# Linear attention with a gated feed-forward on one core: F by the casting queue, first scores ahead of the turns of F, last unit normalised by VectorE

## The chip, the cores and the metric

The kernel runs on one core of one Trainium2 chip. The time is the device time of an execution in microseconds (us); a profile's span is about 1.8 us shorter than the time of the same execution.

## The reference

```python
k_proj = np.einsum('ks,bhsd->bhkd', E, k)            # E, F: [64, 1024], b = h = 8, s = 1024, d = 64
v_proj = np.einsum('ks,bhsd->bhkd', F, v)
scores = scale * np.matmul(q, k_proj.transpose(0, 1, 3, 2))
attn = softmax(scores)                               # over 64 columns
x = np.matmul(attn, v_proj)                          # -> [8192, 512]
g = x @ w_gate; val = x @ w_val                      # 512 -> 1536
out = (g * sigmoid(g) * val) @ w_out                 # 1536 -> 512, float32
```

## The kernel before

The work of one chunk of 512 tokens follows on that of the last; TensorE does attention for a later chunk between feed-forward matmuls. All of that is the same in both kernels. The change touches the prologue, in which nothing is loaded yet. Its parts (cuts marked with `...`):

```python
# loads. nc.sync / nc.scalar: hardware queues. nc.gpsimd: the queue that casts fp32 to bf16
nc.scalar.dma_start(out=kraw[i][:], in_=k[0, 2*i : 2*i+2]...)      # i = 0, 1: heads 0-3, fp32
nc.sync.dma_start(out=Eraw, in_=E); nc.scalar.dma_start(out=Fraw, in_=F)    # fp32 (condensed)
load_q(0, 0, (0, 2)); load_k(0, 4, 8)                              # casting queue
...
load_q(0, 0, (2, 4)); load_v(0, (0, 4, 6, 8)); load_w_gv(0, 1); load_w_gv(1, 2, (0,))
warm(11); turn(0, "v"); warm(4)      # fillers; E turned by TensorE
...
u_KV(0, "k", (0, 4), at="y")         # project k of heads 0-3
u_T(0, 0, "a", act)                  # turn q of unit 0
u_KT0((0, 2), "vg", ...)             # block-diagonal k
turn(1, "a", (0,))                   # F, half 0
u_T(0, 2, "a", act)
u_S(0, 0, "g"); u_R(0, 0); u_N(0, 0) # scores+exp (ACT), row sums (VectorE), normalise (GpSimd)
load_w_gv(1, 2, (1,)); load_w_gv(2, 4, (0,))       # GpSimd issues these behind u_N(0, 0)
...
u_S(0, 2, "g"); u_A(0, 0, dve)       # turn the attention tile of unit 0, copied by VectorE
u_R(0, 2); u_N(0, 2)
u_S(0, 1, "g"); ...; u_N(0, 1); u_S(0, 3, "v"); ...; u_N(0, 3)
u_V0(0, 2, "y"); u_PV2(0, 0, 0, 0, act); ...       # project v, then attention times v
load_w_gv(2, 4, (1,))                # GpSimd: behind u_N(0, 3)
f_mm(0, 0, 0, 0); ...                # first feed-forward matmuls
load_w_gv(4, 6); load_q(0, 1, hs=(0, 4)); load_w_gv(6, 8); ...
```

`load_w_gv(c0, c1)` loads the columns of w_gate and w_val of the feed-forward tiles c0 to c1-1. A chunk uses tile f's w_gate, then w_val, and goes on to f + 1. GpSimd takes its work in order, so a casting DMA waits for the normalisation ahead of it (in the profile before, GpSimd normalises until 20.05 us and its next DMA issue starts at 20.00). A unit is one quarter of the first chunk's attention: four heads, half of the chunk's tokens. A "turn" is a transpose on TensorE, and a piece is the columns that one weight DMA brings.

The softmax here doesn't subtract the row's maximum and nothing guards it: scores larger than these inputs give would overflow.

## Time and profile before

| | before |
|---|---|
| median of the first 3 runs | 569.97 us (569.49 to 570.03) |
| profiled execution | 569.27 us, span 567.5 us |
| TensorE busy | 561.1 us (99%) |
| TensorE 46 to 560 us | 100% |
| granted clock | 0.999 |

The profile's page starts with the busy time per engine. A time line gives one row per group of like instructions: start, duration, engine, source line, operation, output <- input, and in brackets the idle time before it with what ended it. The lists of waits give who waited for whom, total us, times, longest. In these lines PE is TensorE, PEld its weight loads, DVE VectorE, ACT ScalarE, POOL GpSimd, and SPq the queue of SyncE.

### The profile page before, as it was taken

The numbers are of one execution on the slowest core, as the hardware profiler recorded it, in microseconds if no ns is written. First come the engines' busy times: TensorE is split into PE (matmuls) and PEld (weight loads), VectorE is DVE, ScalarE is ACT, GpSimd is POOL, SyncE is SP. The second block draws the span as 40 slices with busy tenths as digits, with TensorE's granted clock in tenths as the row PEclk, the third lists the DMA queues.
The fourth block names the chain that finished last, engine by engine and source line by source line (L and its number), as shares of the span: only waits on it lengthen the run. The fifth ranks groups of instructions, "written<-read, shape, count | busy, mean of one in ns | idle before, by whom it ended". The sixth has DMA issues, their size and how long they took to land.

```text
span 567.5 us, 7942 instructions
## 1 busy us (share of the span) xinstructions
PE 561.1 (99%) x2970; PEld 266.5 (47%) x2970; DVE 338.9 (60%) x576; ACT 235.7 (42%) x416; POOL 111.0 (20%) x124
## 2 busy tenths in 40 slices
PE   8999999999999999999999999999999999999997
PEld 4654444444444444444444444444444444444444
DVE  3786664766476645766466655666547665545550
ACT  3564452444435443443434434354343543443322
POOL 6951250124012400123002230023100220000000
PEclk9999999999999999999999999999999999999999
DMA  9999999729913795029940499106990213101012
GB/s 207 184 199 190 168 146 199 138 57 185 194 49 74 116 198 114 38 57 166 182 80 37 76 185 203 38 19 112 192 180 19 61 39 69 38 37 38 19 38 93
DMA packets 111159, 62.91 MB, mean 111 GB/s; under 512 B 64272, under 2 KB 102416, under 8 KB 111120
## 3 DMA queue, kind: packets, MB, share of 16 engines
q0 software_dynamic: 42816, 29.36, 36.1%
q1 hardware_dynamic: 67392, 31.46, 26.6%
q10 hardware_dynamic: 912, 1.57, 1.0%
q8 instruction: 23, 0.38, 0.3%
q14 instruction: 16, 0.13, 0.1%
HBM read 60.29 MB, written 16.78 MB: 136 GB/s over the span
## 4 chain that ended last, share of the span: by engine, by line
PE 95%; DMA 2%; POOL 1%; DVE 1%; ACT 0%; issue 0%; POOLq 0%
PE yps L415 29%; PE vps L377 28%; PE gps L377 28%; PE kvp L150 3%; PE sc L271 2%; PE pv L328 2%; DMA wv<-in_moe_w_val_dram 2%; PE warm L517 1%; PE efp L505 0%; POOL AA L301 0%; POOL wv L118 0%; POOL wg L118 0%; DVE BD L138 0%; PE kTp L194 0%; PE qTp L237 0%
## 5 line engine op out<-in xcount | busy, mean ns | idle before, releaser
L396 DVE SCALAR_TENSOR_TENSOR s<-th,gps 128x512 f32<-128x512 f32 x192 | 130.4, 679 | 134.6 <-ACT th L389 134.1
L377 PE MATMUL vps<-xT,wv 128*128 128x512 bf16 (+1 forms) x776 | 197.5, 377 | 0.4 <-DMA wv<-in_moe_w_val_dram 0.3
L377 PE MATMUL gps<-xT,wg 128*128 128x512 bf16 (+1 forms) x776 | 197.7, 377 | 0.1
L415 PE MATMUL yps<-wo,hT 128*128 128x512 bf16 (+1 forms) x780 | 194.5, 376 | 0.0
L389 ACT ACTIVATE th<-gps 128x512 f32<-128x512 f32 x192 | 114.6, 597 | 159.0 <-PE gps L377 153.9
L401 DVE TENSOR_TENSOR hT<-s,vps 128x512 bf16<-128x512 f32 x192 | 132.0, 687 | 20.4 <-DVE s L396 0.5
L301 POOL TENSOR_TENSOR AAd<-ee,rr 128x512 bf16<-128x512 f32 x56 | 58.3, 1043 | 342.3 <-issue 184.8
L415 PEld LDWEIGHTS <-hT 128*128 128x128 bf16 x780 | 76.2, 98 | 89.9
L377 PEld LDWEIGHTS <-wv 128*128 128x128 bf16 x776 | 73.8, 98 | 84.2 <-issue 2.9
L377 PEld LDWEIGHTS <-wg 128*128 128x128 bf16 x776 | 74.0, 98 | 81.3 <-issue 1.2
L425 ACT ACTIVATE ysb<-yps 128x512 f32<-128x512 f32 (+1 forms) x65 | 38.4, 591 | 77.7 <-PE yps L415 77.7
L138 ACT CAST xT<-pv 128x512 bf16<-128x512 f32 (+1 forms) x62 | 35.9, 582 | 52.3 <-PE pv L328 50.3
L286 DVE TENSOR_REDUCE zz<-ee 128x8 f32<-128x512 f32 x64 | 43.5, 679 | 22.4 <-ACT ee L275 22.4
L275 ACT ACTIVATE ee<-sc 128x512 f32<-128x512 f32 x64 | 37.9, 595 | 19.7 <-PE sc L271 18.5
L271 PEld LDWEIGHTS <-qTd 128*128 128x128 bf16 x224 | 17.2, 98 | 13.2 <-DMA qTd<-qb 0.2
L328 PE MATMUL pv<-AT,BDV 128*128 128x512 bf16 x60 | 22.4, 379 | 0.1
L271 PE MATMUL sc<-BD,qTd 128*128 128x128 bf16 x224 | 21.6, 219 | 0.0
L288 DVE RECIPROCAL rr<-zz 128x8 f32<-128x8 f32 x64 | 13.0, 203 | 6.7 <-DVE zz L286 0.5
L108 POOL DMA_DIRECT2D qb<-in_q_dram x18 | 16.3, 908 | 1.4 <-POOLq L655 0.8
L150 PE MATMUL kvp<-kb,ET 128*64 128x512 bf16 (+1 forms) x72 | 15.5, 358 | 0.0
L162 DVE CAST BDV<-kvp 64x256 bf16<-64x256 f32 x7 | 3.0, 426 | 20.0 <-ACT ks L158 17.8
L150 PE MATMUL kvp<-vb,FT 128*64 128x512 bf16 x56 | 13.4, 382 | 0.0
(64 smaller groups left out, 137.7 us busy)
## 6 DMA issues: line engine op xcount, KB each, us to landing
out_dram<-ysb SPq DMA_DIRECT2D x63, 256.0 KB, 2.3
qb<-in_q_dram POOLq DMA_DIRECT2D x14, 512.0 KB, 18.0
kb<-in_k_dram POOLq DMA_DIRECT2D x7, 1024.0 KB, 11.0
vb<-in_v_dram POOLq DMA_DIRECT2D x7, 1024.0 KB, 14.4
wo<-in_moe_w_out_dram POOLq DMA_DIRECT2D x2, 768.0 KB, 21.8
wg<-in_moe_w_gate_dram POOLq DMA_DIRECT2D x5, 256.0 KB, 8.0
wv<-in_moe_w_val_dram POOLq DMA_DIRECT2D x5, 256.0 KB, 9.6
kraw<-in_k_dram ACTq DMA_DIRECT2D x2, 512.0 KB, 4.9
```

What stands on the lines that cost most here:

```text
L138: (nc.scalar.copy if eng is nc.scalar else eng.tensor_copy)(out=out, in_=in_)
L150: nc.tensor.matmul(out=t[lo : lo + 64, h0:h1].rearrange("p h d -> p (h d)"), lhsT=w[:, j, :], rhs=src[b][:, h0:h1, j, :], start=(j == 0), ...
L271: nc.tensor.matmul(out=ps[:, n, :], lhsT=t[:, n, :], rhs=BD[b % 2][:, 4 * g + n, :], start=True, stop=True)
L275: nc.scalar.activation(out=e[:].rearrange("p h j k -> p (h j k)"), in_=ps[:].rearrange("p a k -> p (a k)"), func=AF.Exp, scale=scale,)
L286: nc.vector.reduce_sum(out=z[:], in_=e[:], axis=AX.X)
L301: eng.tensor_tensor(out=a.rearrange("p j h k -> p h j k"), in0=ee.pop((b, u))[:], in1=rr.pop((b, u))[:].unsqueeze(3).to_broadcast([P, 4, 2 ...
L377: nc.tensor.matmul(out=ps[:, ts], lhsT=(wg, wv)[w][:, kt, f * P : (f + 1) * P], rhs=x[:, kt, ts], start=(kt == 0), stop=(kt == NKT - 1),)
L389: nc.scalar.activation(out=th[:], in_=ps[:], func=AF.Tanh, scale=0.5)
L396: nc.vector.scalar_tensor_tensor(out=s1[:], in0=th[:], scalar=1.0, in1=g[:], op0=ALU.add, op1=ALU.mult)
L401: nc.vector.tensor_tensor(out=hT[c][:, f, :], in0=s1[:], in1=ps[:], op=ALU.mult)
L415: nc.tensor.matmul(out=yy[c][:, cs], lhsT=hT[c][:, f, i * P : (i + 1) * P], rhs=wo[:, f, cs], start=(f == 0), stop=(f == NFT - 1),)
L425: nc.scalar.activation(out=ysb[:, cs], in_=yy[c][:, cs], func=AF.Copy, scale=0.5)
```

## The change

Four intents: the fp32 load of F leaves ACT's hardware queue and comes as bf16 by the casting queue, between q and v, so that k, E and q land sooner; F's turns move behind the second scores, where they no longer hold up the first exp; the last of the four normalisations goes to VectorE, so that GpSimd is through earlier; and the copy of the first attention tile moves from VectorE to ACT.

```diff
-        ef = []
-        for which, src in (("E", E), ("F", F)):
-            raw = const.tile([KP, S], FP32, name=f"{which}raw")
-            (nc.sync if which == "E" else nc.scalar).dma_start(out=raw[:], in_=src)
-            ef.append(raw)
+        ef = [const.tile([KP, S], dt, name=f"{n}raw") for n, dt in (("E", FP32), ("F", BF16))]
+        nc.sync.dma_start(out=ef[0][:], in_=E)
...            # turn(): PSUM tile and identity in bf16 for F
         load_q(0, 0, (2, 4))
+        nc.gpsimd.dma_start(out=ef[1][:], in_=F)
         load_v(0, (0, 4, 6, 8))
...
         u_KV(0, "k", (0, 4), at="y")
-        warm(1)
         u_T(0, 0, "a", act)
         u_KT0((0, 2), "vg", (dve, dve, dve, act))
-        turn(1, "a", (0,))
-        u_T(0, 2, "a", act)
+        warm(1)
         u_S(0, 0, "g")
...
-        turn(1, "a", (1,))
-        warm(1)
+        u_T(0, 2, "a", act)
+        warm(2)
         u_KV(0, "k", (4, 8), at="y")
...
         u_S(0, 2, "g")
-        u_A(0, 0, dve)
         u_R(0, 2)
         u_N(0, 2)
+        turn(1, "a", (0,))
         u_S(0, 1, "g")
         u_R(0, 1)
         u_N(0, 1)
+        turn(1, "a", (1,))
         u_S(0, 3, "v")
         u_R(0, 3)
-        u_N(0, 3)
+        u_A(0, 0, act)
+        u_N(0, 3, dve)
...            # one warm(1) less; u_A(0, 1, dve) and u_A(0, 3, act) a few places earlier
```

More of the change, by code (lines that the diff above doesn't have):

```diff
@@ L501, in turn @@
             for half in halves:
-                ps = bank(at, [P, 4, KP], FP32, "efp")
+                ps = bank(at, [P, 4, KP], (FP32, BF16)[which], "efp")
                 for i in range(4):
-                    j = 4 * half + i
                     nc.tensor.transpose(
                         out=ps[:, i, :],
-                        in_=ef[which][:, bass.ds(j, P, step=NJ)],
-                        identity=ident_fp[:KP, :KP],
+                        in_=ef[which][:, bass.ds(4 * half + i, P, step=NJ)],
+                        identity=(ident_fp, ident_bf)[which][:KP, :KP],
                     )
@@ L562 @@
         u_N(0, 1)
+        turn(1, "a", (1,))
         u_S(0, 3, "v")
         u_R(0, 3)
-        u_N(0, 3)
+        u_A(0, 0, act)
+        u_N(0, 3, dve)
         u_V0(0, 2, "y")
         u_PV2(0, 0, 0, 0, act)
-        warm(1)
         u_V0(2, 3, "y")
@@ L572 @@
         u_PV1(0, 0, 2, 0, dve)
+        u_A(0, 1, dve)
         u_PV1(0, 0, 3, 0, act)
-        u_A(0, 1, dve)
+        u_A(0, 3, act)
         load_w_gv(2, 4, (1,))
         f_mm(0, 0, 0, 0)
-        u_A(0, 3, act)
         u_PV2(0, 0, 0, 1, dve)
```

## The prediction

> **What bounds the kernel now.** I read the page's list of busy times first, then the busy tenths, then TensorE's waits, then the time line of the start. The page of the kernel before:
>
> ```profile
> span 567.5 us, 7942 instructions
> ...
> PE 561.1 (99%) x2970; PEld 266.5 (47%) x2970; DVE 338.9 (60%) x576; ACT 235.7 (42%) x416; POOL 111.0 (20%) x124
> ```
>
> TensorE is busy for 99% of the span, so 567.5 - 561.1 = 6.4 us are left, and some of those 561 us are fillers ("warm" matmuls that keep the clock up). Where TensorE waits for a named thing (waits of TensorE, whole span; us in total, times, longest):
>
> ```profile
> PE warm L517 <- DVE zeros L495: 1.2, 1, 1.2
> PE pv L343 <- ACT BDV L185: 0.5, 1, 0.5
> PE vps L377 <- DMA wv<-in_moe_w_val_dram: 0.3, 1, 0.3
> PE pv L355 <- ACT AT L138: 0.2, 1, 0.2
> ```
>
> All lie before 22 us. The busy table by stages gives TensorE 100% of every stretch from 46 us to 560 us. That part is a fixed amount of work: what the change can gain, it gains before some 35 us, and the rest moves as a block. So the question is what sets the pace there. The time line of TensorE has these starts (start us, us, then the group; the last bracket is idle time and what ended it):
>
> ```profile
> 12.47 1.06 PE L150 MATMUL kvp<-kb,ET 128*64 128x256 bf16 x8
> ...
> 21.21 0.61 PE L377 MATMUL vps<-xT,wv 128*128 128x256 bf16 x4 [0.30 <-DMA wv<-in_moe_w_val_dram]
> 21.66 0.60 PE L377 MATMUL gps<-xT,wg 128*128 128x256 bf16 x4
> ```
>
> The 21.21 start waited for the first piece of w_val. I worked out each landing from the DMA view in windows around one issue (issue plus time to landing): E 6.04, k heads 0-3 4.64 and 6.14, first q 9.55, F 8.97, k heads 4-7 11.81, second q 13.31, v 15.81, 17.06, 18.12, then wg/wv: 19.15, 21.19, 21.51, 22.25, 23.55, 24.90, 26.30, 27.94. TensorE uses the second to fourth of the weight pieces at 21.21, 21.66 and 22.32, that is 0.02, 0.15 and 0.07 us after they landed. The chain of waits in the first 46 us says the same a little later:
>
> ```profile
> 19.02 1.03 POOL AA L301
> 20.05 0.76 POOL wv L118
> 20.81 0.75 POOL wg L118
> ...
> 23.74 9.64 DMA wv<-in_moe_w_val_dram
> 33.38 0.05 issue
> 33.43 1.04 PE vps L377 x4
> ```
>
> The wv columns for tiles 6 and 7 land at 33.4 us, and the matmul that needs them starts at 33.43. TensorE's queue was free for it at about 33.15 (the four 128-column transposes before it start at 32.93 and take 4 x 0.055), so 0.28 us is lost there. After it, pieces land 1.3 us apart (34.3, 35.7, 37.0, 38.4, 39.7) and are used later than that. **The start is bounded by the DMA engines, with TensorE at most 0.3 us behind them**: the DMA row of the page shows 9s from 2.5 us on.
>
> **What the Trainium skill says.** "DMA: Bandwidth & Descriptors", section "Issuing engines are not separate DMA queues": DMAs started by different engines run on the same 16 DMA engines and interleave, so moving an issue saves only issue time. The trace agrees: while the ACT/SP queues still moved fp32 (7 to 9 us) everything together ran at 204 GB/s with the casting queue sharing, and the casting queue alone runs at 209 GB/s of bf16 in 9 to 11 us, which is 418 GB/s read. "Runtime: NRT & Kernel Launch", section "Instruction fetch mechanics": programs are fetched in blocks of 16 KiB (256 instructions) by the engine's own DMA queue, with a cost said to be mostly hidden. The trace has 23 such packets; two lie at 19.1 and 31.3 us and take one DMA engine 0.94 us each, and just there two landings come late (wv at 21.19, 2.04 us after its neighbour; wv at 33.4, 2.7 us after its neighbour, against 1.3 us elsewhere). So it is not hidden here, by my reading. "SBUF — State Buffer", section "Who interferes with whom": a VectorE instruction with two inputs in SBUF and a GpSimd instruction that reads SBUF exclude each other. The trace before has no such pair at the start, so it can neither agree nor differ; it bears on the last part of the change.
>
> **The change part by part.**
>
> 1. *F by the casting queue.* It leaves ACT's queue (issue 0.54 us, free there) and costs GpSimd one issue more (0.75 us, between q and v at 5.0 us, with over 10 us of transfers queued, so hidden). For the DMA engines: 262 KB less among the early fp32 loads. In 6 to 8 us these moved 417 KB of fp32 and 135 KB of bf16 (270 KB read), 343 KB read per us, so F took 262/343 = 0.76 us; in the casting queue 131 KB at 209 KB/us = 0.63 us. E, k and both q land about 0.6 us sooner; v and all weights 0.1 us sooner. F itself lands at 13.3 - 0.6 + 0.6 = 13.3 or so, against 8.97; its first turn now stands behind the second scores, at about 14.5. The landings are 8 deep in semaphores (the ninth casting DMA waits for the first: GpSimd's 9.81 us issue waited 1.05 us for q), so wv's first piece is issued near 9 instead of 8 us: hidden, too.
>
> 2. *Turning F in bf16.* 2 x 4 fp32 transposes take 0.65 us per four (rows at 10.01 and 11.57), bf16 ones 0.39 by the model and 0.22 in pitch. About 0.6 us of TensorE goes, one warm matmul (0.22) comes ahead of the first scores, one more before the second k, two go elsewhere. So the first half loses 1.2 us of turns and gains 0.4 of fillers.
>
> 3. *First scores ahead.* Before, scores 0 end at 11.64 and their exp starts at 12.03, because ACT first did an FT cast (0.37) and a q copy (0.59). Now the exp starts at about 11.35 (q's turn 0.3 us earlier without the warm ahead of it). The second k projection started at 12.47 with its data landed at 11.81; now it can start near 12.0. So scores 2 and their exp come about 0.5 us sooner (15.3 to 14.8).
>
> 4. *A(0,0) off VectorE.* One copy of 0.41 us stood ahead of the second reduction (15.57 to 15.98). With the 0.5 us above, GpSimd's second normalisation starts near 16.2 to 16.3 instead of 17.01.
>
> 5. *Last unit on VectorE.* GpSimd's three normalisations take 3.04 us (17.01 to 20.05), and its DMA issues stand behind them. Now two: 16.3 to 18.3. VectorE takes the third (0.69 us, the duration of its tensor_tensor on 128x512) at about 17.9, or 18.3 to 19.0 if the two exclude each other. The wv issue of 20.0 moves to about 18.4. The DMA rate fell from 195 to 157 GB/s in 24 to 26 us, when the pieces issued late were due: (195 - 157) x 2 us = 76 KB, plus some 60 KB in the neighbouring microseconds, about 0.7 us of transfer that an earlier issue may give back.
>
> 6. *What ACT pays.* It now has two FT casts among the exps (2 x 0.37, less overlap 0.6 us) and the A(0,0) copy (0.59, about 0.5 in pitch) between the last exp and the BDV copies. Exps end at 14.8 + 1.6 + 0.6 = 17.0, as before (16.9), and the chain BDV, xT, AT, BDV, PV after them is 0.5 us later. Carried through (BDV 17.9, A(0,2) turned 18.75 and copied 19.65, last BDV 19.9, xT 20.7, first f matmuls to 20.95), TensorE reaches the first wv matmul at 21.2, where before it could at 20.9.
>
> **The sum.** At 21 us: wv lands 0.1 us sooner and TensorE is about level with it, 0 to -0.1 us. At 33.4 us: up to 0.28 us of wait can go if the piece lands 0.3 or more sooner, which 0.1 + up to 0.7 us makes likely; TensorE's own pace then binds. Together -0.1 to -0.4 us, of 570. Centre: 569.97 - 0.3 = 569.65.
>
> **The rivals.** (a) *Hidden anyway*: everything waits for the weights as before, change 0 to -0.1, 569.9. For it: three landings used within 0.15 us. (b) *ACT becomes the bound at 17 to 21 us*: TensorE reaches wv later than it lands, +0.2 to +0.5, 570.3. For it: step 6; against: ACT is idle for 0.4 to 0.6 us in four places there. (c) *GpSimd's queue was the bound*: the chain runs through its normalisations, and releasing 1.6 us of it shows at 33.4 in full: -0.8, 569.2. Against: TensorE is busy up to 33.15 and can't be there much sooner. (d) *Instruction fetch falls elsewhere*: 14 more TensorE instructions move the two 0.94 us fetches to other pieces, ±0.4 us.
>
> **Range and chances.** Three runs before spread by 0.5 us. The rivals give 569.2 to 570.3; with 0.3 us of noise on either side, 568.9 to 570.4. A change of 2% is 11.4 us, twice all of TensorE's idle time; only a stall outside this reasoning could do it, so 0.99 for within 2%.
>
> **What would show it.** Right: TensorE still 100% busy from 36 us; second k projection at 12.0; GpSimd's normalisations done by 18.5; first wv matmul at 21.0 to 21.3 and the one on tiles 6 and 7 at 32.9 to 33.3; DMA above 170 GB/s in 24 to 26 us. Wrong: turns of F waiting for their transfer (an in-order queue would hold scores 1 and 3), VectorE's normalisation stalled well past 19 us, or a gain or loss over 1 us, which would mean that I misread what sets the pace before 33 us.

## The result, and the profile after

The changed kernel took 568.68 us (median of 4, 568.62 to 568.87); the kernel before took 569.73 us (median of 4 runs, the first three and one more, 569.02 to 570.03). The difference of the medians is 1.05 us. The ratio is 0.9984, with a 95% interval of 0.9967 to 1.0001. A ratio here is the mean time of one kernel's fast runs over that of the other's of the same rounds, so it is not quite the ratio of the medians. The change is within 2%, as expected, but the time lies 0.2 us under the range given. Expected were 0.3 us; the medians differ by 1.05 us, the two profiled executions by 0.60 us.

The page of the changed kernel:

```profile
span 566.9 us, 7938 instructions
...
PE 560.2 (99%) x2970; PEld 266.3 (47%) x2970; DVE 339.2 (60%) x576; ACT 236.0 (42%) x417; POOL 110.4 (19%) x124
```

TensorE's waits, whole span:

```profile
PE warm L513 <- DVE zeros L492: 1.2, 1, 1.2
PE sc L271 <- DVE BD L138: 0.7, 1, 0.7
PE pv L343 <- ACT BDV L185: 0.7, 1, 0.7
PE pv L355 <- ACT AT L138: 0.2, 1, 0.2
```

No wait for w_val is left, and the one for ACT's BDV copy (the block-diagonal v) grew from 0.5 to 0.7 us. A new wait of 0.7 us is for the block-diagonal k (BD) that VectorE copies: with F's turns gone from there, TensorE stands still, and the first scores start at 10.90 us in place of 11.02, only 0.12 us sooner. TensorE's time line:

```profile
12.11 1.06 PE L150 MATMUL kvp<-kb,ET 128*64 128x256 bf16 x8
...
20.70 0.60 PE L377 MATMUL gps<-xT,wg 128*128 128x256 bf16 x4
...
21.36 0.60 PE L377 MATMUL vps<-xT,wv 128*128 128x256 bf16 x4
...
33.29 1.03 PE L377 MATMUL vps<-xT,wv 128*128 128x512 bf16 x4
```

The second k projection starts 0.36 us sooner than before, but the first w_val matmul 0.15 us later (21.36 against 21.21): what the order of the scores gained, ACT's longer queue took back. The w_val matmul of tile 6 starts 0.14 us sooner (33.29 against 33.43). That is all the prediction spoke of. From there to the last matmul both profiles run alike: lined up from the end, every matmul of the changed kernel starts 0.14 to 0.15 us sooner, and TensorE ends at 563.90 us in place of 564.05. But the spans differ by 0.6 us. **The other 0.44 us lie behind TensorE's end**: 567.49 - 564.05 = 3.44 us before, 566.90 - 563.90 = 3.00 us after. I call that stretch the tail.

What happens there shows in the waits of SyncE's queue. Before:

```profile
SPq L666 <- DMA out_dram<-ysb: 3.6, 1, 3.6
```

After:

```profile
SPq L662 <- DMA out_dram<-ysb: 3.2, 3, 1.3
```

L666 and L662 are the end of the program, where SyncE waits for all DMAs. Before it waits once, for 3.6 us; after, three times, 3.2 us in all. The trace's records of these waits tell the rest (when each of SyncE's waits ended, us from TensorE's end, by the number of the semaphore):

```
before  sem 106: -1.53   107: 2.10   109: 2.17   111: 2.23   113: 2.29   115: 2.35   116: 2.41   117: 2.47   118: 2.53
after   sem 106: -1.53   107: -1.47  109: -1.40  111: -1.34  114: -1.27  115: -1.21  116: 0.11   117: 1.43   118: 2.09
last output DMA (96 KB, issued at 0.40 in both): signals semaphore 107 before, 118 after
```

SyncE goes through its semaphores in a fixed order and spends 0.06 us on each. Eight of the numbers belong to hardware DMAs, which take them in turn. In the trace there are 97 hardware DMAs before (64 of SyncE, 28 transposes, 5 of ACT) and 96 after, because F's left. Divided by 8, 97 leaves a remainder of 1: the last output, the one that everybody waits for, has the first semaphore, and seven waits that are long fulfilled stand behind it. 96 leaves none: it has the last. 2.53 - 2.09 = 0.44 us.

### The profile page after: what moved, and what is told of

Same layout as the page of the kernel before. It is cut to its first block, busy times and chain, and to the rows that moved or that the text cites. A ratio compares the mean times of both kernels' runs of the same rounds, so it can differ in the third digit from the quotient of the medians.

```text
span 566.9 us, 7938 instructions
## 1 busy us (share of the span) xinstructions
PE 560.2 (99%) x2970; PEld 266.3 (47%) x2970; DVE 339.2 (60%) x576; ACT 236.0 (42%) x417; POOL 110.4 (19%) x124
## 4 chain that ended last, share of the span: by engine, by line
PE 97%; ACT 1%; DVE 1%; issue 0%
PE gps L377 29%; PE yps L415 29%; PE vps L377 29%; PE kvp L150 3%; PE sc L271 2%; PE pv L328 2%; PE warm L513 1%; ACT ee L275 0%; ACT AT L138 0%; DVE BD L138 0%; ACT th L389 0%; PE qTp L237 0%; PE efp L501 0%; PE aTp L317 0%; PE pv L343 0%
## 5 line engine op out<-in xcount | busy, mean ns | idle before, releaser
L108 POOL DMA_DIRECT2D qb<-in_q_dram x18 | 16.3, 907 | 1.4 <-POOLq L651 0.8
## 6 DMA issues: line engine op xcount, KB each, us to landing
wo<-in_moe_w_out_dram POOLq DMA_DIRECT2D x2, 768.0 KB, 21.9
```

## The experiments

Each kernel ran beside the kernel before on the same chip. The medians of the kernel before ran from 569.11 to 569.73 us over the rounds, so runs of the same rounds are compared; where the text compares across rounds, it says so. Every kernel gave a correct result. This table has the numbers of each profile: the first feed-forward matmul of full width (its start fixes everything after it that does not wait), the landing of the w_val piece of tiles 6 and 7, its first use, and TensorE's end. Without a wait, the use comes 8.2 us behind the first full-width matmul. A landing is the issue plus the time to landing, which the view gives in tenths, so it is good to 0.05 us.

| profile | time of it | first full-width | piece lands | its use | TensorE ends | tail |
|---|---|---|---|---|---|---|
| before | 569.27 | 24.94 | 33.34 | 33.43 | 564.05 | 3.44 |
| before_again | 568.93 | 24.88 | 31.88 | 33.09 | 563.70 | 3.42 |
| before_look1 | 569.19 | 25.11 | 32.39 | 33.33 | 563.98 | 3.44 |
| before_look2 | 569.54 | 25.06 | 33.65 | 33.70 | 564.33 | 3.44 |
| before_look3 | 569.57 | 24.93 | 33.50 | 33.53 | 564.35 | 3.44 |
| after | 568.67 | 25.07 | 31.35 | 33.29 | 563.90 | 3.00 |
| after_again | 568.83 | 25.24 | 31.13 | 33.45 | 564.07 | 2.99 |
| after_third | 568.74 | 25.16 | 31.45 | 33.37 | 563.98 | 2.99 |
| only_dve_norm | 569.04 | 24.97 | 31.36 | 33.19 | 563.80 | 3.44 |
| before_early_issue_again | 569.11 | 25.05 | 31.47 | 33.27 | 563.88 | 3.43 |
| before_plus7 | 568.66 | 24.92 | 31.96 | 33.14 | 563.88 | 3.00 |
| before_dve_plus7 | 568.87 | 25.19 | 31.53 | 33.41 | 564.08 | 3.01 |
| after_gpsimd_norm | 568.69 | 25.08 | 31.36 | 33.29 | 563.90 | 2.99 |
| after_late_issue2 | 569.53 | 25.06 | 33.84 | 33.89 | 564.75 | 3.01 |
| after_plus1 | 569.09 | 25.07 | 31.26 | 33.28 | 563.89 | 3.42 |
| after_F_act | 569.63 | 25.60 | 31.59 | 33.81 | 564.42 | 3.43 |
| after_A0_dve | 568.39 | 24.80 | 31.21 | 33.02 | 563.63 | 2.99 |
| after_A0_dve_again | 568.90 | 25.22 | 31.81 | 33.43 | 564.14 | 3.00 |

### First round: both kernels again, and VectorE's normalisation alone, put in and taken out

before_again is the kernel before, after_again and (later) after_third the changed kernel.

> The kernel before once more. Both theories expect 1.000 against itself; it measures how far two builds of the same kernel differ. The late-issue theory also expects that the wait at the w_val piece of tiles 6 and 7 (0.28 us in the first profile, at 33.4 us) varies from profile to profile, since that piece lands just as it is needed; the chance theory (the difference is in the last writes after TensorE's end, 3.4 us before and 3.0 us after) expects that wait to be the same and the tail to vary.

> The changed kernel once more, for an interval that is narrow enough. Late-issue theory: 0.9 to 1.2 us faster than before, and no wait for any w_val piece after 22 us. Chance theory: between 0 and 0.5 us.

```diff
# only_dve_norm, on the kernel before
-        u_N(0, 3)
+        u_N(0, 3, dve)
# after_gpsimd_norm, on the changed kernel
-        u_N(0, 3, dve)
+        u_N(0, 3)
```

> The kernel before with one edit: the last unit is normalised by VectorE. Late-issue theory: GpSimd's casting DMAs of 20.0 us come at about 19.0, the DMA rate in 24 to 26 us rises from 157 towards 195 GB/s, the piece of tiles 6 and 7 lands before 33.0 us, and most of the gain is there: -0.6 to -1.0 us. Theory that the moved F or the earlier scores are the cause: 0 to -0.2 us.

> The changed kernel with one edit: the last unit goes back to GpSimd. Late-issue theory: the issue of 18.6 us moves to about 19.7, still 0.3 us earlier than before, the dip of the DMA rate comes back in part, and 0.5 to 1.0 us of the gain is lost. Theory of F or of the earlier scores: at most 0.2 us lost.

Before: 569.23 us (9 runs, 568.74 to 570.87). before_again: 569.15 (568.93 to 569.36), ratio 0.9995. after_again: 568.83 (568.60 to 568.88), ratio 0.9988 (0.9976 to 1.0001). only_dve_norm: 569.13 (569.04 to 569.49), ratio 0.9996. after_gpsimd_norm: 568.69 (568.65 to 568.80), ratio 0.9987.

The late-issue theory failed here as it stood: VectorE's normalisation gains 0.1 us at most when put in, and loses nothing when taken out. The step behind it did happen. The busy table of 24 to 26 us has as its last column the DMA rate (GB/s). Kernel before:

```profile
24.00:26.00 2.00, 1.90 (x13) 1.08 (x12) 1.70 (x3) 0.76 (x2) 2.00 (x4) 1.00 1.25 157
```

only_dve_norm:

```profile
24.00:26.00 2.00, 1.90 (x14) 1.12 (x12) 1.67 (x3) 0.80 (x2) 1.88 (x3) 1.00 1.44 195
```

The dip goes and the piece lands at 31.36 us, but a piece that lands at 31.9 us is early enough too, as before_again shows: its use at 33.09 us did not wait. before_again also speaks against the chance theory, which expected the same wait and another tail: the wait was gone and the tail was 3.42 us again. after_again's gain of 0.40 us is less than the late-issue theory expected. All profiles of the first two kernels fell into two classes by the tail, and after_gpsimd_norm, which lacks VectorE's part, kept the short one. That led to the next theory, on the number of hardware DMAs.

### Second round: the end of the program

```diff
# after_plus1: n = 1, on the changed kernel; before_plus7: n = 7, on the kernel before; behind the load of E
+        tiny = const.tile([n, 16], FP32, name="tiny")
+        for i in range(n):
+            nc.sync.dma_start(out=tiny[i : i + 1, :], in_=E[i : i + 1, 0:16])
```

> The changed kernel with one more tiny DMA (64 bytes) on SyncE's hardware queue at the start, whose result nobody reads. End-of-program theory: hardware DMAs take 8 completion semaphores in turn, SyncE waits for the 8 in a fixed order at the end, some 0.06 us each; the last output's semaphore, last in the order in the changed kernel, becomes the first again as in the kernel before. So the tail after TensorE's end grows from 3.00 to 3.44 us and the time by 0.4 us. Theory that the 0.44 us of tail come from the moved F itself or from chance: tail 3.00 and the time as the changed kernel.

> The kernel before with seven such tiny DMAs, 7 being one less than 8. End-of-program theory: tail 3.00 instead of 3.44 us, time -0.4 us; the seven cost nothing (SyncE's queue is free there), unless their place behind E disturbs the first loads. Chance theory: no change.

after_plus1: 569.14 us (569.08 to 569.15, and one of 571.07 at a mean clock of 0.997), ratio to the kernel before 1.0006: the gain is gone. before_plus7: 568.66 (568.53 to 569.06), ratio 0.9992 (0.9980 to 1.0005), against 569.11 for the kernel before in the same rounds: 0.45 us gained by seven loads that nobody reads. The intervals of the ratios include 1, so the times alone would not show it. The profiles do: the tails are 3.42 and 3.00 us, and TensorE's ends are those of the parent kernels within the scatter of the table. SyncE's wait in after_plus1:

```profile
SPq L665 <- DMA out_dram<-ysb: 3.6, 1, 3.6
```

and in before_plus7:

```profile
SPq L669 <- DMA out_dram<-ysb: 3.2, 3, 1.3
```

In all 18 profiles of the table the tail is 3.42 to 3.44 us where the count of hardware DMAs leaves a remainder of 1 by 8 and 2.99 to 3.01 us where it leaves 0. This part is settled.

### Second round: the issue alone, and ACT's copy

```diff
# before_early_issue (and before_early_issue_again), on the kernel before
         load_w_gv(2, 4, (0,))
+        load_w_gv(2, 4, (1,))
...
-        load_w_gv(2, 4, (1,))
# after_A0_dve (and after_A0_dve_again), on the changed kernel
         u_S(0, 2, "g")
+        u_A(0, 0, dve)
...
-        u_A(0, 0, act)
```

> The kernel before, with the issue of w_val's tiles 2 and 3 put ahead of GpSimd's second normalisation instead of behind the fourth (16.3 instead of 20.0 us), so that all later casting DMAs come some 0.7 us sooner. Late-issue theory: the piece of tiles 6 and 7 lands near 31.4 us, ahead of the instruction fetch of 31.4 us, in place of 31.9 to 33.3; the wait at 33.1 to 33.4 us is gone and the runs spread by under 0.4 us (before: 568.7 to 570.9). Tail 3.44. Median -0.1 to -0.3 us. If the spread stays, late issue is not its cause.

> The changed kernel with the copy of the first turned attention tile back on VectorE and in its old place. Theory that ACT's extra 0.5 us made TensorE late at 21 us (20.7 instead of 19.75 us for the first f matmul): that matmul at 20.2 us or before, the first w_val matmul at 21.2 or as its data lands, and the time -0.15 to -0.25 us against the changed kernel. If the weights' landing binds anyway: no change.

before_early_issue: 569.23 us (568.95 to 570.48), ratio 0.9999. Its profile is of the run of 570.48 us at a mean clock of 0.996 and says nothing of the question: TensorE was idle for 1.3 of the microseconds 4 to 8, the clock was 0.57 from 8 to 12 us, and all that follows came 1.4 us late. The other four runs lie within 0.32 us (568.95 to 569.27). Such runs (570.1 to 571.1 us, clock 0.996 to 0.997) occurred four times, once each in the kernel before, in after_plus1, here and in the repetition. before_early_issue_again repeats it, below.

after_A0_dve: 568.46 us (568.39 to 568.82), ratio 0.9989 (0.9976 to 1.0001), the lowest median of all. In its profile the first w_val matmul starts at 21.08 us, 0.28 us sooner than in the changed kernel; E's turn, with which TensorE's chain starts, came 0.07 us sooner, so 0.21 us are due to the edit. The first feed-forward matmul came at 20.43 us, later than the 20.2 expected.

### Third round: the copy again, F back, and the fetch

> The changed kernel, to stand beside the next in the same rounds. Tail 3.0 us; 0.5 us under the kernel before.

> The changed kernel with the first attention tile copied by VectorE, again. It was 0.2 to 0.4 us under the changed kernel, of other rounds. If ACT's extra 0.5 us at 17 us costs TensorE, it is 0.2 to 0.4 us under it here too; if that was chance, they are equal.

```diff
# after_F_act, on the changed kernel; the turns in fp32 again, in their new place
-        ef = [... (("E", FP32), ("F", BF16))]
+        ef = [... (("E", FP32), ("F", FP32))]
         nc.sync.dma_start(out=ef[0][:], in_=E)
+        nc.scalar.dma_start(out=ef[1][:], in_=F)
...
-        nc.gpsimd.dma_start(out=ef[1][:], in_=F)
# before_fetch_later, on the kernel before; warm32: the same fillers in fp32, half as wide
-        warm(11); turn(0, "v"); warm(4)
+        warm(3); warm32(4); turn(0, "v"); warm32(2)
```

> The changed kernel with F back on ACT's hardware queue in fp32, turned in fp32, in its new place among the scores. The hardware DMAs are one more again. End-of-program theory: tail 3.44 us, +0.44 us. Theory that F's transfer itself speeds the start: E, k and q land 0.6 to 0.9 us later and the first f matmuls come later by more than 0.2 us, so +0.6 us or more in all. If F's place is hidden: +0.4 us and no more.

> The kernel before with 12 of its 15 first filler matmuls replaced by 6 fp32 ones of half the width (about the same time, fewer instructions), so that TensorE's instruction fetch of 31.3 us comes about 1 us later. Fetch theory: the w_val piece of tiles 6 and 7 then always lands at 31.9 us instead of 31.9 to 33.3, no wait at 33 us in the profile, and the runs spread by 0.3 us or less apart from those of a lower clock. If the runs still spread from 568.6 to 569.6, the fetch is not what spreads them. The start may shift by a few tenths, as the fillers do not last exactly as long.

Before: 569.63 us (9 runs, 568.95 to 569.65). after_third: 568.74 (568.67 to 568.84), ratio 0.9987 (0.9975 to 1.0000). after_A0_dve_again: 568.61 (568.44 to 568.90), ratio 0.9984 (0.9970 to 0.9997). The copy on VectorE is 0.13 us under the changed kernel by the medians of the same rounds, but the runs overlap. In its profile E landed at 6.34 us and not at 6.04, which put the whole chain 0.28 us back: E's turn at 6.47, the first w_val matmul at 21.50, a distance of 15.03 us, against 21.44 - 6.20 = 15.24 us in after_third. So the edit shortens TensorE's chain by 0.21 us, as in the first try. The profiled run, at 568.90 us, is the slowest of the five. That the time follows when E lands on time is likely (after_A0_dve), not shown.

after_F_act: 569.99 us (569.63 to 570.17), ratio to the kernel before 1.0008; against after_third it loses 1.25 us. 0.44 us are the tail (3.43 us). In the profile, another 0.44 us lie in the start: q lands at 9.65 in place of 8.44 us and TensorE waits 0.4 us for it, and the fp32 turns of F, now between the scores, put the last scores back from 15.98 to 16.56 us. The profiled run is the fastest of the five, and where the others lose up to 0.5 us more is not shown. In this profile, then, F's new place among the scores is good only with F in bf16 by the casting queue.

before_fetch_later: 569.25 us (569.21 to 569.88), ratio 0.9999. It did not test what it was meant to: the fetch moved by 0.3 us only (31.63 against 31.31 us), since the 6 fp32 fillers are 12 matmuls in the trace, as many as they replaced. Its piece landed at 32.74 us, in time, in this one profile, although the fetch had begun 1.1 us before. Inconclusive.

### Fourth and fifth round: how the kernel before waits

> The kernel before, one profile. If the spread of its runs is the wait for the w_val piece of tiles 6 and 7: time = 568.65 us + 0.1 + that wait + whatever comes before it, so an execution of 569.6 us shows a wait near 33 us of about 0.6 us or a later start of the feed-forward part by as much, and one of 569.0 shows none. If the waits are the same whatever the time, the spread is elsewhere.

> As before_look1: a second profile of the kernel before on this chip.

> A further profile of the kernel before. A time of 569.0 to 569.2 goes with no wait for the piece of tiles 6 and 7, 569.3 or more with a wait at 33 us; tail 3.44 us.

```diff
# after_late_issue2, on the changed kernel: last unit on GpSimd, and one useless normalisation behind it
-        u_N(0, 3, dve)
+        u_N(0, 3)
+        nc.gpsimd.tensor_tensor(out=spare[:], in0=e1[:], in1=r1..., op=ALU.mult)
```

> The changed kernel with the last unit back on GpSimd and one more, useless, normalisation behind it, so that the w_val piece of tiles 2 and 3 is issued at 20.7 us instead of 18.6 and later than in the kernel before (20.0). Late-issue theory: the piece of tiles 6 and 7 lands at 32.5 to 33.5 us, the wait at 33 us is there, and the time is 0.2 to 1.0 us over the changed kernel's 568.7, with a spread. If the issue has slack anyway: 568.7 to 568.8.

> The kernel before with the piece of tiles 2 and 3 issued ahead of the second normalisation, again. Late-issue theory: at full clock the profile shows the piece of tiles 6 and 7 landed by 31.9 us and no wait at 33 us; runs 568.9 to 569.2 where the kernel before has up to 569.65. Else: as the kernel before.

```diff
# before_dve_plus7, on the kernel before
+        tiny = ...; seven loads as in before_plus7
...
-        u_N(0, 3)
+        u_N(0, 3, dve)
```

> The kernel before with two edits alone: the last unit normalised by VectorE, and seven tiny hardware DMAs. If the end of the program and the late piece are the whole: tail 3.0 us, the piece of tiles 6 and 7 landed before 32 us, 568.6 to 568.75 us and a spread like the changed kernel's, without F by the casting queue and without the new order of scores. If F or the order give more: 0.2 us or more above the changed kernel's 568.7.

The three looks took 569.19, 569.54 and 569.57 us. By the table, the first had no wait at 33 us, the other two had it: their piece landed at 33.65 and 33.50 us. In before_look2 TensorE's time line reads

```profile
33.05 0.39 PE L237 MATMUL qTp<-ident_bf,qb 128*128 128x128 bf16 x4
33.70 1.04 PE L377 MATMUL vps<-xT,wv 128*128 128x512 bf16 x4 [0.26 <-DMA wv<-in_moe_w_val_dram]
```

and 33.70 - 25.06 = 8.64 us in place of 8.2, so the piece cost 0.43 us. Over the five profiles of the kernel before, TensorE's end lies 538.8 and 538.9 us behind the first full-width matmul in the two without a wait, and 539.1, 539.3 and 539.4 us in the three with one: a loss of 0 to 0.6 us by the run. The piece itself cost 0.28, 0.43 and 0.38 us of these; in before_look3 another 0.2 us were lost later.

after_late_issue2: 569.38 us (568.88 to 569.84), ratio to the kernel before 0.9999, where the changed kernel had 0.9984 to 0.9988 and 568.7 us in other rounds. So the changed kernel's gain is gone, although the short tail is kept (3.01 us). after_gpsimd_norm, which has the first of its two edits, lost nothing. Its profile:

```profile
33.05 0.39 PE L237 MATMUL qTp<-ident_bf,qb 128*128 128x128 bf16 x4
33.89 0.82 PE L377 MATMUL vps<-xT,wv 128*128 128x512 bf16 x3 [0.45 <-DMA wv<-in_moe_w_val_dram]
```

Issued at 20.62 us, w_val's tiles 2 and 3 started a row of late pieces; the DMA rate of 24 to 26 us was 130 GB/s, and the piece of tiles 6 and 7 landed at 33.84 us. The wait and the spread came back. So late issue does bring the wait. Issued at 19.64 us (after_gpsimd_norm) the piece is in time, at 20.0 to 20.3 us (kernel before) it goes either way, at 20.62 us it is late; the first and the last are one profile each.

Late issue alone does not make the wait, though. In the table's profiles the piece just ahead in the queue, w_gate of tiles 6 and 7, landed at 29.8 to 31.2 us, and at the usual distance of 1.3 to 1.4 us even the latest would have brought w_val in time (at 32.6 us, where the use without a wait comes at 33.0 us or later). The wait is there only in the four profiles in which w_val came 2.5 to 2.9 us after it (before, before_look2, before_look3, after_late_issue2). In these four an instruction fetch of TensorE had begun 0.5 to 1.0 us before the piece was due. Where the issue was early, the piece had landed before the fetch began, or within 0.2 us of it. But in before_again, before_look1, before_plus7 and before_fetch_later a fetch had begun 0.4 to 1.1 us before the landing too, and the piece was in time. So an early issue takes the piece out of the stretch in which it can be delayed; what delays it there, in some runs and not in others, is not shown.

before_early_issue_again: 569.19 us (569.00 to 570.06), ratio 0.9999. Its piece landed at 31.47 us and was not waited for, as expected, but one run of 570.06 us is there. That run is of the lower clock (0.996); the other four lie at 569.00 to 569.20 us, as expected, where the kernel before has 568.87 to 569.62 (median 569.38). Over the two tries the four runs at full clock spread by 0.2 and 0.3 us, the nine of the kernel before by 0.8 and 0.9; the median came 0.19 us lower once and 0.12 us higher once. So an earlier issue shows in the landing and the spread, and not clearly in the median.

before_dve_plus7: 568.87 us (568.51 to 569.24) against 569.16 for the kernel before (9 runs), ratio 0.9994 (0.9980 to 1.0008). The tail is 3.01 us, the piece landed at 31.53 us. With these two edits 0.29 us were gained, less than the tail's 0.44 alone, and without the small spread of the changed kernel. The changed kernel gained 0.40 to 1.05 us in other rounds and did not run in these, so whether the two edits are the whole is not shown. Its profile lost time earlier, in a wait for the w_gate piece of tile 1, which landed at 21.82 us:

```profile
21.91 0.61 PE L377 MATMUL gps<-xT,wg 128*128 128x256 bf16 x4 [0.45 <-DMA wg<-in_moe_w_gate_dram]
```

Over the table's ten profiles in which F comes by ACT's queue that piece landed at 21.3 to 21.9 us, over the eight with F by the casting queue at 21.1 to 21.7, some 0.2 us sooner on average. The moved F may thus help the start; no run isolates it.

## Why the prediction was right or wrong

**What sets the pace before 35 us: right for the kernel before.** TensorE stayed fully busy from there to 560 us, and the pieces landed 1.3 us apart. In the changed kernel TensorE waits for no weight any more, so its own chain sets the pace. Two readings were off. The second fp32 pair of k landed at 7.25 us, not at 6.14: the view gave the median of two issues. And that TensorE takes the first w_val piece 0.02 us after it landed is one draw: in before_look1 to before_look3 it landed at 20.0 to 20.2 us and was used at 21.0 to 21.1.

**Steps 1 to 5 on their own: mostly right, steps 3 and 4 in part.** F landed at 13.10 us (13.3 expected) and hindered nothing, the second k projection started at 12.11 (12.0), scores 0's exp at 11.56 (11.35; TensorE had to wait for BD), GpSimd was through its normalisations at 18.68 (18.3) and issued at 18.63 (18.4). Its second normalisation started at 16.64, where 16.2 to 16.3 was expected: 0.37 of the 0.75 us hoped for. E and the second k pair hardly came sooner (5.98 and 7.20 against 6.02 and 7.25 us), q and the second half of k by 0.9 to 1.2, v and the first w_gate by 0.3. The rate of 24 to 26 us rose to 196 GB/s. VectorE's normalisation was mis-sized: 1.13 us, not 0.69 (VectorE's rows, changed kernel):

```profile
18.10 1.13 DVE L301 TENSOR_TENSOR AA<-ee,rr 128x512 bf16<-128x512 f32 x1
```

Nobody waited for it: the tile was turned at 20.48 us, and VectorE itself was idle from 19.23 to 20.01 us.

**Step 6, ACT pays: right, and with it rival (b) in its mechanism, at the low end of its 0.2 to 0.5 us.** The first w_val matmul started at 21.36 us, 0.15 us later than before, and TensorE no longer waited for data there. Putting the copy back on VectorE gave back 0.21 us.

**The sum before 35 us: right for the pair of profiles, in part by luck.** TensorE's end came 0.15 us sooner, in the range of 0.1 to 0.4, but the start came 0.15 us later where 0 to 0.1 us sooner was expected, and the wait at 33.4 us happened to cost 0.28 us in the profile before. I took that wait from one profile; it cost 0 to 0.43 us by the run. I saw that the landing was tight and did not ask how it would scatter. On average over the profiles the first full-width matmul comes about 0.2 us later (24.98 us before, 25.16 after), and about 0.3 us less are lost behind it. Rival (c) put the full 1.6 us of GpSimd's earlier release at the end of the chain; the runs show only the wait itself. The range's upper end was added up wrongly: 570.3 + 0.3 is 570.6.

**The step that failed: "the rest moves as a block".** The prediction took all behind 46 us as a fixed amount of work and never looked behind TensorE's last matmul. There the change took 0.44 us, more than all its intended parts on average: over the profiles, TensorE's end is 564.08 us before (mean of five) and 563.98 after (mean of three), a gain of 0.10 us, and the tail fell from 3.44 to 2.99. The cause, one hardware DMA less, stands in the first lines of the diff. By the medians the whole difference was 1.05, 0.40 and 0.89 us in the three rounds with the unchanged kernels side by side. The prediction's sign for a misreading of the pace before 33 us, a change over 1 us, came true in the first of them; the profiles show that the pace was not what had been misread.

**Rival (d), the fetch: the reason was wrong.** "14 more TensorE instructions" came from counting rows of the program. The traces have 2970 matmuls and 2970 weight loads in both kernels, and the two fetches stayed nearly in place (19.14 and 31.31 us before, 19.14 and 31.55 after).

**What stays open.** The profiles account for 0.54 us (0.44 in the tail, 0.10 before it). The slowest runs of the kernel before (569.97, 570.03 us) were not profiled, and their clock is not on record; that their excess is the same wait is likely, not shown. Whether the instruction fetch at 31.3 us decides if the piece lands at 31.9 or at 33.5 us is open too: it coincides in every late case and in some that are not late, and the one run meant to move it failed to. What the moved F alone is worth to the start was not isolated.

**A better version.** The changed kernel with the first tile's copy back on VectorE (after_A0_dve) had the lowest median in both its rounds, 568.46 and 568.61 us, the second 0.13 us under the changed kernel beside it.

## What to carry to other kernels

When TensorE is busy to the end, look behind its end as well: the stretch from the last matmul to the end of the span is as real as any wait, and a change in the number of DMAs can move it without touching the data. Where a transfer lands just as it is needed, one profile shows one draw; take several before sizing the wait, and the gain of an earlier issue may be a smaller spread rather than a steady shift, as here. Work moved to another engine to free one queue should be followed through that other queue to the next point where the two meet: here ACT's 0.5 us ate what the earlier scores gave.

## What the Trainium skill lacked or had wrong

- End of the program (no page has it; "Runtime: NRT & Kernel Launch" gives one figure for the barrier of all engines at the end): hardware DMAs take 8 completion semaphores in turn, SyncE waits for them in a fixed order, 0.06 us each, so the last DMA's place among the 8 is worth up to 0.44 us (tail 2.99 to 3.01 against 3.42 to 3.44 us in all profiles).
- "Runtime: NRT & Kernel Launch", section "Instruction fetch mechanics", calls the cost of a fetch mostly hidden. The page speaks of the instruction stream and says nothing of data transfers beside it. Each 16 KiB packet took one DMA engine 0.89 to 0.95 us here, and beside a busy casting queue pieces landing just then came up to 2.9 us after their neighbours in place of 1.3, in four of the eight profiles in which a fetch had begun 0.4 us or more before w_val of tiles 6 and 7 was due. The coincidence is shown, the cause is not.
- "SBUF — State Buffer", section "Who interferes with whom": the exclusion of a VectorE instruction with two SBUF inputs and a reading GpSimd instruction agrees with the runs. In all nine profiles with it, VectorE's normalisation started 0.33 to 0.58 us before the end of GpSimd's and ended 0.55 us after it, whenever it had started, so it took 0.88 to 1.13 us; GpSimd's kept its 1.03 us. Missing on the page is a figure for the loss.
